# Scan and expert layer on one core: runs of eight in the corner products, split copies, six loads in flight, zero rows by GpSimd, and a new list

## The chip, the cores and the metric

One core of a Trainium2 chip runs the whole program. The metric is device microseconds of one execution. Three executions of the kernel before took 586.05, 586.7 and 592.21 us; the median is 586.7 us.

## The reference

The reference is a recurrent attention over 768 time steps for 4 batches and 8 heads of 40 channels, followed by a mixture of experts. Per step and head it keeps a 40 x 40 state:

```python
y[t] = r[t] @ state
Sa = state @ a[t]
state = state * w[t] - outer(Sa, b[t]) + outer(v[t], k[t])
```

The outputs of all heads form 3072 rows of 320 columns. Each row goes to the expert with the largest logit (8 experts with 320 x 1024 and 1024 x 320 weights, ReLU between, a capacity of 768 rows each), and its result is weighted by the softmax probability of that expert.

## The kernel before

The scan is done in 6 blocks of 128 steps (index `i`), each for two halves of the batches (`pr` = 0, 1) and in two chunks of 64 steps (`c` = 0, 1). Within a chunk the recurrence is a triangular system. A block has these steps, named as in the list:

- `load_w`, `load_a`, `load_kb`, `load_rv`, `load_v` (L457 to L495 and `unit`) bring the block's inputs into the buffers `px`, `a`, `kb`, `rv` and `vu`. Each such step is two DMAs, issued by SyncE (SP) through `Schedule.dma` (L156). The first load into a buffer has 128 rows, whose last rows are zeros in memory; a later load into the same buffer has 112 rows (the set `whole` remembers the buffers that have had a full load). Loads are spaced: each DMA waits until the third DMA before it has landed.
- `decay` scans `px` twice on VectorE (L503, L512) and multiplies `a` (L517); `decay_k` multiplies the two halves of `kb` (L522). The second half reads the last column of `gx`, which GpSimd sets to one (L427).
- `nn` and `kk` are products of `kb` and `a` on TensorE; their results are copied to `ns` and, masked, to `tk`.
- `inverse` (L587 to L830) inverts the triangular matrices: a transposition of `ns` (L791), a chain of small eliminations on VectorE (L638, L643), two corner products that are each two multiplications (L661) and a sum (L668, L670), and two transpositions (L680, L685). `unit` sets the buffer `nu` to the identity on ScalarE and reads a column of ones from `few`, which GpSimd sets (L434).
- `join`, `lower`, `lower_w` and `comb` join the inverted parts with products on TensorE. `take_n` makes four masked copies from `n1` to `yb` and `take_n1` two; both are one step in the list, on one engine.
- `chain`, `uT`, `turn`, `out`, `zz`, `iden` carry the state from chunk to chunk; `gate`, `logi`, `rout` prepare the routing.

The experts follow (`x`, `w`, `p`, `h`, `o` in the list), with weights loaded and split while the last blocks run, and take the last 200 us.

All steps are emitted in the order that `ORDER` gives, one text list for all engines, and each engine runs its own instructions in that order. In the list `name*2` is two steps of a name, `name/1` the second choice of engine for it (VectorE instead of ScalarE for copies, GpSimd instead of VectorE for multiplications), and `name~9` puts nine warm-up matmuls (L196, on TensorE, 128 x 512, whose results nobody uses) ahead of it. Instructions outside the list, as the memsets at the start (L425 to L445), are ordered by a planner, in the text's order unless one isn't ready. Before the first step the text clears buffers: PSUM on ScalarE, then on GpSimd the columns of the four `vu` buffers that `load_v` writes later, then `D`, `E`, `yq`, `yb`, `zs`, then the column of `gx`, then `mask` and `few`:

```python
    clear(*[flat(x) for x in free_["pp"] + free_["p1"]])
    for x in [x[:, :, :, C:3 * C] for x in free_["vu"]] + free_["D"] + free_["E"] + free_["yq"] + free_["yb"] + free_["zs"]:
        G.memset(x, 0.0)
    for x in free_["gx"]:
        G.memset(x[:, H * (P + 1):], 1.0)
...
            dma(U["vu"][half(x ^ pr), x, :, C:3 * C], vt[pr, q, x].rearrange("p (k y) -> p k y", k=4))
```

## Time and profile before

| what | value |
|---|---|
| median of three executions | 586.7 us (586.05 to 592.21) |
| the profiled execution | 590.8 us, span 589.1 us |
| TensorE busy | 521.2 us, 88% |
| VectorE busy | 413.9 us, 70% |
| ScalarE busy | 293.5 us, 50% |
| GpSimd busy | 160.8 us, 27% |
| mean granted TensorE clock | 0.992 |

The span is the time from the first to the last instruction of the profiled execution; some 1.7 us lie around it. A busy share is a mean over stages: the start (to about 57 us), the scan (to about 380 us) and the experts. In a timeline each row is a group of like instructions of one engine with its start and the time it covers; what stands in brackets is how long the engine stood idle before and what released it. PE is TensorE, PEld its weight loads, DVE VectorE, ACT ScalarE, POOL GpSimd, SP SyncE; SPq is the queue on which SP issues DMAs.

### The profile page before, as it was taken

The page shows a single profiled execution, that of the slowest core. Times are in us where ns is not written, and L with a number is a line of the kernel's source. Part 1 is how long each engine was busy: PE and PEld are TensorE (multiplying, and loading weights), DVE is VectorE, ACT ScalarE, POOL GpSimd, SP SyncE. Part 2 cuts the span into 40 slices and gives each one's busy share as a digit, 9 for nine tenths or more (in the row PEclk, how much of TensorE's full clock was granted, in tenths as well). Part 3 has the DMA queues.
Part 4 walks back from the last instruction along what each step waited for, and adds up shares of the span by engine and source line. Part 5 has one row for each costly group of instructions (what it writes and reads, how often), then busy time and mean ns, then how long its engine had stood idle before and what let it go on. Part 6 is the DMA issues. An engine that isn't in the chain of part 4 may idle for free.

```text
span 589.1 us, 24793 instructions
## 1 busy us (share of the span) xinstructions
PE 521.2 (88%) x11162; PEld 383.8 (65%) x11162; DVE 413.9 (70%) x665; ACT 293.5 (50%) x550; POOL 160.8 (27%) x181
## 2 busy tenths in 40 slices
PE   0587898999989899999798999799899999999994
PEld 0354477877877887878687788566665465555653
DVE  5886889779896988798899879657247256363340
ACT  3333656572786577357634453445345445273231
POOL 9014102340240223233202000412444441423203
PEclk9998999999999999999899999999999999999999
DMA  7754005332661534254221313675998877693301
GB/s 230 216 177 151 3 5 164 116 120 72 195 196 41 172 119 143 68 168 141 89 78 46 119 48 125 165 216 170 210 225 183 271 175 172 150 267 117 83 22 59
DMA packets 74760, 80.81 MB, mean 137 GB/s; under 512 B 31550, under 2 KB 55232, under 8 KB 74644
## 3 DMA queue, kind: packets, MB, share of 16 engines
q1 hardware_dynamic: 71316, 69.69, 41.4%
q0 software_dynamic: 3328, 9.44, 5.5%
q8 instruction: 89, 1.46, 1.0%
q14 instruction: 27, 0.22, 0.1%
HBM read 64.16 MB, written 10.09 MB: 126 GB/s over the span
## 4 chain that ended last, share of the span: by engine, by line
issue 20%; PE 15%; DVE 7%; POOL 6%; DMA 4%; ACT 2%; SPq 1%; POOLq 1%; DVEq 0%; ACTq 0%
PE pp L403 5%; PE pp L1624 3%; POOL out_dram L1499 3%; PE p L1493 3%; POOL a L1470 2%; DMA xT<-a 1%; DMA a<-xd,ri 1%; PE pp L885 1%; DMA out_dram<-tk,ri 1%; DVE vu L455 1%; DMA nt<-in_moe_w_dram 1%; DVE yq L661 1%; PE p L1126 1%; PE pp L570 1%; SPq L1609 1%
## 5 line engine op out<-in xcount | busy, mean ns | idle before, releaser
L522 POOL TENSOR_TENSOR kb<-kb,gx 104x1024 f32<-104x1024 f32 x13 | 33.4, 2576 | 80.7 <-DMA kb<-in_kb_dram 47.3
L196 PE MATMUL pp<-ident 128*128 128x512 f16 x148 | 41.8, 397 | 12.2 <-ACT pp L421 3.2
L403 PE MATMUL pp<-a,kb 64*64 64x64 f32 x1536 | 31.3, 229 | 20.9 <-DVE a L517 18.5
L403 PEld LDWEIGHTS pp<-a,kb 64*64 64x64 f32 x1536 | 26.8, 140 | 30.6 <-DVE a L517 21.0
L1470 POOL DMA_INDIRECT a<-xd,ri x26 | 30.3, 1166 | 58.3 <-DVE gs L1385 31.3
L1499 POOL DMA_INDIRECT out_dram<-tk,ri x23 | 25.9, 1126 | 61.3 <-ACT tk L1659 49.4
L403 PE MATMUL pp<-vu,bk 128*40 128x104 f32 (+1 forms) x768 | 38.2, 252 | 3.3 <-DVE vu L455 3.2
L143 ACT COPY vT<-pp 128x1024 f32<-128x1024 f32 x21 | 21.3, 1014 | 31.4 <-PE pp L885 28.7
L403 PEld LDWEIGHTS pp<-vu,bk 128*40 128x40 f32 x768 | 32.8, 117 | 6.1 <-DVE vu L455 4.3
L503 DVE TENSOR_TENSOR_SCAN gx<-px,z 104x1032 f32<-104x1032 f32 x12 | 29.2, 2430 | 8.5 <-DMA px<-in_w_dram 6.9
L517 POOL TENSOR_TENSOR a<-a,px 104x1024 f32<-104x1024 f32 x8 | 17.5, 2182 | 55.6 <-DVE px L512 30.1
L1624 PE MATMUL pp<-xT,z 128*128 128x448 f16 (+2 forms) x128 | 27.7, 306 | 5.4 <-DMA xT<-a 4.3
L1624 PE MATMUL pp<-xT,ns 128*128 128x448 f16 (+2 forms) x192 | 32.1, 306 | 0.0
L455 DVE TENSOR_TENSOR vu<-pp,mask 128x1024 f32<-128x1024 f32 x22 | 26.7, 1213 | 7.0 <-PE pp L403 4.9
L147 ACT ACTIVATE ns<-pp 32x256 f32<-32x256 f32 (+1 forms) x45 | 20.2, 449 | 22.3 <-PE pp L403 21.2
L143 ACT COPY zs<-pp 64x320 f32<-64x320 f32 x46 | 19.3, 419 | 23.9 <-PE pp L403 23.4
L196 PEld LDWEIGHTS <-ident 128*128 128x128 f16 x169 | 15.0, 100 | 24.1 <-issue 12.0
L403 PE MATMUL pp<-rv,vT 64*64 64x64 f32 x1536 | 28.4, 221 | 2.5 <-issue 1.3
L451 POOL TENSOR_SCALAR_AFFINE_SELECT tk<-tk 64x512 f32<-64x512 f32 x20 | 14.5, 726 | 57.5 <-ACT tk L448 46.6
L578 ACT ACTIVATE bk<-pp,few 128x320 f32<-128x320 f32 x48 | 22.5, 528 | 14.8 <-PE pp L570 14.5
L403 PE MATMUL pp<-yb,ns 128*64 128x64 f32 (+1 forms) x768 | 25.8, 229 | 3.7 <-ACT yb L147 3.6
L403 PEld LDWEIGHTS pp<-rv,vT 64*64 64x64 f32 x1536 | 24.9, 134 | 5.9 <-issue 2.2
(267 smaller groups left out, 1426.4 us busy)
## 6 DMA issues: line engine op xcount, KB each, us to landing
vu<-in_moe_w_dram SPq DMA_DIRECT2D x32, 320.0 KB
kb<-in_kb_dram SPq DMA_DIRECT2D x40, 224.0 KB
rv<-in_rv_dram SPq DMA_DIRECT2D x24, 256.0 KB
vu<-in_vt_dram SPq DMA_DIRECT2D x48, 128.0 KB
px<-in_moe_w_dram SPq DMA_DIRECT2D x12, 512.0 KB
xd<-x SPq DMA_DIRECT2D x24, 192.0 KB
px<-in_moe_w_dram SPq DMA_DIRECT2D x16, 256.0 KB
a<-in_a_dram SPq DMA_DIRECT2D x16, 224.0 KB
```

What stands on the lines that cost most here:

```text
L143: (e.copy if e is self.nc.scalar else e.tensor_copy)(out, in_)
L147: (e.mul if e is self.nc.scalar else e.tensor_scalar_mul)(out, in_, x)
L196: self.nc.tensor.matmul(x, self.spare[:, 0:P], self.spare[:, None, :].to_broadcast([P, 2, 2 * P]), start=True, stop=True, skip_group_check ...
L403: TT.matmul(out, l, r, start=start, stop=True, skip_group_check=True)
L455: V.tensor_mul(out, in_, m.to_broadcast(sh))
L503: V.tensor_tensor_scan(T["gx"][0:R, 0:H * (P + 1)][:, ::-1], T["px"][0:R].rearrange("p h t -> p (h t)")[:, ::-1], z2[0:R].rearrange("p h t ...
L522: engine().tensor_mul(x, x, g[:, :, None, half(c)].to_broadcast([R, H, 2, C]))
L578: A.activation(U["bk"][:, x].rearrange("p (a b) d -> p a b d", a=2), U["pi"][:, :, 0:4 * R].rearrange("p a (b y) -> p a b y", y=R)[:, :, : ...
L1470: nc.gpsimd.indirect_dma_start(out=xt(j)[:c].rearrange("p a c -> p (a c)"), out_offset=None, in_=src[:, :], in_offset=bass.IndirectOffsetO ...
L1493: nc.tensor.matmul(po[z], h(l, f + z), rr(f + z, 1)[:, 0], start=(f == 0 and m == 0), stop=(f == NF - n and m == 2), skip_group_check=True)
L1499: nc.gpsimd.indirect_dma_start(out=out_v[used[0] % (8 * E)][:, :], out_offset=bass.IndirectOffsetOnAxis(ap=ri.bitcast(U32)[:c, j, 1:2], ax ...
L1624: nc.tensor.matmul(s_["h", f + z][:, :n], l, rr, start=m % 7 == 0 and m < 14, stop=m >= 14)
```

## The change

- The first corner product is laid out anew and a step `corner_turn` is added to `inverse`: VectorE copies the 128 elements that the product reads in strides of 32 into `tmp`, in rows of eight. Both corner products then read all operands in runs of eight neighbouring elements; the second one is reordered in the same way.
- `take_n` and `take_n1` are two steps each, of half the copies, which the list can put on different engines.
- The first 24 load DMAs wait for the sixth before them instead of the third.
- Eight buffers (the four of `a`, one of the two of `kb`, three of the six of `px`) count as filled from the start, so that their first loads have 112 rows too; GpSimd sets rows 96 to 127 of each to zero, in the text just ahead of the memsets of `vu`.
- The list is a new one for the whole program: 1812 steps for 1794 (18 more, from the split and the added steps), and 146 warm-up matmuls for 169.

```diff
--- before.py
+++ after.py
 ORDER = """
-load_kb load_w decay0 load_kb load_a decay0 load_rv load_kb load_w decay_k0 load_a load_kb inverse_0 load_w decay_k0
-decay1 decay0 nn0~1 nn0 nn0~9 decay1 decay_k1 load_v decay1 kk decay_k1 decay0 unit nn0 nn1*2 kk/1 nn1 load_a
...
+load_w load_v unit load_kb decay0 decay_k0 load_w load_kb*2 decay0 decay_k0 load_rv load_w load_a decay1 load_a
+decay0 nn0 decay1 inverse_0 load_kb nn0 nn0~12 decay_k1 decay1 kk nn0 decay_k1 nn1*2 kk/1 decay0 nn1*2 inverse*2
+kk~3 iden1~4 inverse load_v iden0~3 iden0 inverse load_a iden1 inverse load_v kk/1 inverse*3 iden1~5 load_a inverse
+load_w inverse*3 load_rv inverse iden1 inverse*2 iden0 inverse*2 zz0~5 inverse*2 zz1~10 inverse*2 chain1 join_sw
+join/1 join decay0 load_kb decay_k0/1 join~9 load_kb decay0 iden0 decay_k0 join join~7 join*2 lower comb load_kb*2
+lower comb/1 comb~12 nn0~4 load_w decay1 comb/1 lower_w comb~5 tk_ decay1 decay_k1 inverse_0 nn0 decay1 comb nn0~6
+comb nn0 nn1~2 decay_k1 decay0 nn1 load_g nn1~3 nn1 unit chain1 chain0/1 chain0~2 kk inverse chain0 inverse*2 uT0~1
+inverse*2 load_w chain1 inverse uT0 inverse*4 kk/1 inverse*2 uT1 out0 uT1 zz0~1 out0/1 inverse out1~1 inverse out0
+inverse out1/1 out1 inverse out0 chain0 out0 out1 load_v turn0 out1 load_v chain0 inverse load_a iden0 chain0 zz1
...
@@ -156,8 +157,9 @@
     def dma(self, out, in_):
         x = (self.nc.scalar if self.queue.pop(0) == "A" else self.nc.sync).dma_start(out, in_)
         if self.spaced:
-            if len(self.loads) > 2:
-                self.tc.add_manual_dep(x.ins, self.loads[-3].name, LANDED, reason="loads are spaced")
+            n = 6 if len(self.loads) < 24 else 3
+            if len(self.loads) >= n:
+                self.tc.add_manual_dep(x.ins, self.loads[-n].name, LANDED, reason="loads are spaced")
             self.loads.append(x.ins)
 
     def load(self, fn):
@@ -421,6 +423,8 @@
                 A.copy(y, tmp[:, None, 0:256].to_broadcast(list(y.shape)))
 
     clear(*[flat(x) for x in free_["pp"] + free_["p1"]])
+    for x in free_["a"][:1] + free_["kb"][1:] + free_["px"][1:2] + free_["a"][1:2] + free_["px"][2:4] + free_["a"][2:]:
+        G.memset(flat(x)[96:], 0.0)
     for x in [x[:, :, :, C:3 * C] for x in free_["vu"]] + free_["D"] + free_["E"] + free_["yq"] + free_["yb"] + free_["zs"]:
         G.memset(x, 0.0)
     for x in free_["gx"]:
@@ -455,6 +459,8 @@
             V.tensor_mul(out, in_, m.to_broadcast(sh))
 
     whole = set()
+    for x in free_["a"][:1] + free_["kb"][1:] + free_["px"][1:2] + free_["a"][1:2] + free_["px"][2:4] + free_["a"][2:]:
+        whole.add(id(x))
 
     def prep(pr, i):
         T = {"pr": pr, "i": i}
@@ -647,18 +653,24 @@
         def eight(x, b, t, s, *dims):
             return skew(x, b * 528 + t * 32 + s, *dims)
 
+        def corner_turn():
+            V.tensor_copy(tmp[:, 0:P].rearrange("p (b j s) -> p b j s", b=2, j=8),
+                          skew(s_["nu"], 0, (528, 2), (1, 8), (32, 8)))
+
         def corner_mul(x):
             def go():
                 if x == 0:
                     s_["y"] = get("yq")
                 for b in range(2):
+                    y = flat(s_["y"])[:, 512 * b:512 * b + 512]
                     if x == 0:
-                        l = eight(s_["xu"], b, 8, 0, (32, 8), (0, 8), (1, 8))
-                        r = eight(s_["nu"], b, 0, 0, (0, 8), (1, 8), (32, 8))
+                        V.tensor_mul(y.rearrange("p (j t s) -> p j t s", j=8, t=8),
+                                     eight(s_["xu"], b, 8, 0, (0, 8), (32, 8), (1, 8)),
+                                     skew(tmp, 64 * b, (8, 8), (0, 8), (1, 8)))
                     else:
-                        l = eight(s_["nu"], b, 8, 8, (32, 8), (0, 8), (1, 8))
-                        r = skew(tmp, P + 64 * b, (0, 8), (1, 8), (8, 8))
-                    V.tensor_mul(flat(s_["y"])[:, 512 * b:512 * b + 512].rearrange("p (t j s) -> p t j s", t=8, j=8), l, r)
+                        V.tensor_mul(y.rearrange("p (t j s) -> p t j s", t=8, j=8),
+                                     eight(s_["nu"], b, 8, 8, (32, 8), (0, 8), (1, 8)),
+                                     skew(tmp, P + 64 * b, (0, 8), (8, 8), (1, 8)))
             return go
 
         def corner_sum(x):
@@ -691,12 +703,13 @@
             for z in range(2):
                 scale(two(y, z), x(z).rearrange("p (u x) t -> p u x t", x=2), mlo[:, z:z + 1])
 
-        def take_n():
-            y = s_["yb"] = get("yb")
-            for x in range(2):
-                for z in range(2):
-                    o = C // 2 * x + 16 * z
-                    scale(y[half(x), :, o:o + 16], s_["n1"][half(x), :, 0:16], mlo[half(x), z:z + 1])
+        def take_n(x):
+            if x == 0:
+                s_["yb"] = get("yb")
+            y = s_["yb"]
+            for z in range(2):
+                o = C // 2 * x + 16 * z
+                scale(y[half(x), :, o:o + 16], s_["n1"][half(x), :, 0:16], mlo[half(x), z:z + 1])
 
         def turned():
             return [(z, pr, pr * 16 + u, u) for u in range(16) for pr in range(2) for z in range(2)]
@@ -746,11 +759,12 @@
             for pr in range(2):
                 scale(x[half(pr)], s_["ntd"][half(1 - pr), pr * 16:pr * 16 + 16, :], mlo[half(1 - pr), 1:2])
 
-        def take_n1():
-            y = s_["yb"] = get("yb")
-            for x in range(2):
-                scale(y[half(x), :, 32 * x:32 * x + 32], s_["n1"][half(x)], mlo[half(x), 0:1])
-            put("nu", s_["nu"])
+        def take_n1(x):
+            if x == 0:
+                s_["yb"] = get("yb")
+            scale(s_["yb"][half(x), :, 32 * x:32 * x + 32], s_["n1"][half(x)], mlo[half(x), 0:1])
+            if x:
+                put("nu", s_["nu"])
 
         def comb_a():
             p = s_["p"] = get("pp")
@@ -797,6 +811,7 @@
         for s in range(1, ne - 1):
             for x in elim(s):
                 add(x, "V.2")
+        add(corner_turn, "V.4")
         for x in range(2):
             add(corner_mul(x), "V1.2", take=["yq"] * (1 - x))
             add(corner_sum(x), "V1.2", free=["yq"] * x)
@@ -805,7 +820,8 @@
         add = steps("join_sw")
         add(take_sw, "A.33 A.33|V.34 V.34", needs=[("ntd0", i)], take=["sw"], gives=("sw", i))
         add = steps("join")
-        add(take_n, "A.62 A.62 A.62 A.62|V.69 V.69 V.69 V.69", needs=[("n0", i)], take=["yb"])
+        for x in range(2):
+            add(lambda x=x: take_n(x), "A.62 A.62|V.69 V.69", needs=[("n0", i)], take=["yb"] * (1 - x))
         add(join_a, "P1.1", take=["pp"], free=["yb"])
         add(take_ja, "A.62 A.62|V.69 V.69", take=["yq"], free=["pp"])
         add(join_b, "P1.0", needs=[("sw", i)], take=["pp"], free=["yq", "sw"])
@@ -815,7 +831,8 @@
             steps("lower")(lambda pr=pr: lower(pr), "A.62 A.62|V.69 V.69", needs=[("ntd", i)], take=["nt"], gives=("lower", pr, i))
         steps("lower_w")(lower_w, "A.62 A.62|V.69 V.69", needs=[("ntd", i)], take=["sw"], gives=("lower", 2, i))
         add = steps("comb")
-        add(take_n1, "A1.04 A1.04|V1.2 V1.2", needs=[("n1", i)], take=["yb"], free=["nu"])
+        for x in range(2):
+            add(lambda x=x: take_n1(x), "A1.04|V1.2", needs=[("n1", i)], take=["yb"] * (1 - x), free=["nu"] * x)
         add(comb_a, "P1.3", take=["pp"], free=["yb"])
         add(take_a, "A1.04|V1.2", take=["yq"], free=["pp", "ns"])
         add(comb_b, "P1.4", needs=[("lower", x, i) for x in range(3)], take=["pp"], free=["yq", "sw"])
```

## Rows read from the trace of the kernel before

**Rows 1.** The page: busy time, share of the span and instructions by engine.
```profile
PE 521.2 (88%) x11162; PEld 383.8 (65%) x11162; DVE 413.9 (70%) x665; ACT 293.5 (50%) x550; POOL 160.8 (27%) x181
```

**Rows 2.** Table by stages: stage, length, busy of PE, PEld, DVE, ACT, POOL, PEclk, DMA, GB/s.
```profile
0.00:21.00 21.00, 0.88 (x13) 0.40 (x16) 12.48 (x16) 5.22 (x6) 14.44 (x58) 1.00 0.73 234
...
57.00:100.00 43.00, 36.44 (x1139) 28.30 (x1133) 37.28 (x52) 24.79 (x45) 2.18 (x1) 1.00 0.15 42
...
sum 323.00, PE 295.51 PEld 246.93 DVE 277.15 ACT 184.79 POOL 69.17; mean PE 49.25 PEld 41.15 DVE 46.19 ACT 30.80 POOL 11.53
```

**Rows 3.** Timeline of POOL at the start: start, length, engine, line, operation, tiles.
```profile
4.14 0.94 POOL L425 MEMSET vu<- 128x1024 f32 x1
...
5.07 2.72 POOL L425 MEMSET vu<- 128x1024 f32 x3
...
10.47 1.80 POOL L425 MEMSET yb<- 128x2048 f32 x1
...
12.79 0.09 POOL L427 MEMSET gx<- 128x1 f32 x1
```

**Rows 4.** Timeline of DVE, 0 to 32 us.
```profile
6.28 2.31 DVE L503 TENSOR_TENSOR_SCAN gx<-px,z 104x1032 f32<-104x1032 f32 x1 [3.85 <-DMA px<-in_w_dram]
...
12.91 1.23 DVE L522 TENSOR_TENSOR kb<-kb,gx 104x1024 f32<-104x1024 f32 x1 [0.33 <-POOL gx L427]
...
17.23 2.31 DVE L503 TENSOR_TENSOR_SCAN gx<-px,z 104x1032 f32<-104x1032 f32 x1 [3.07 <-DMA px<-in_w_dram]
19.45 1.20 DVE L517 TENSOR_TENSOR a<-a,px 104x1024 f32<-104x1024 f32 x1
...
31.06 1.98 DVE L791 STREAM_TRANSPOSE xu<-ns 128x1024 f32<-128x1024 f32 x1 [1.08 <-ACT ns L147]
```

**Rows 5.** Timeline of SP's DMA queue: the first load and the first of vu.
```profile
0.82 0.88 SPq L157 DMA_DIRECT2D kb<-in_kb_dram  x2
...
21.50 1.32 SPq L157 DMA_DIRECT2D vu<-in_vt_dram  x2
```

**Rows 6.** Timeline of PE: warm-up matmuls of the start.
```profile
21.77 4.02 PE L196 MATMUL pp<-ident 128*128 128x512 f16 x9
...
32.43 2.33 PE L196 MATMUL pp<-ident 128*128 128x512 f16 x10
```

**Rows 7.** Timeline of ACT: the masked copies of block 0.
```profile
47.31 2.68 ACT L147 ACTIVATE yb<-nu,few 64x512 f32<-64x512 f32 x4 [0.47 <-DVE nu L685]
...
60.53 2.32 ACT L147 ACTIVATE yb<-nu,few 64x1024 f32<-64x1024 f32 x2
```

**Rows 8.** DMA view, 0 to 80 us: GB/s in 40 slices of 2 us.
```profile
GB/s 6 316 245 255 244 257 279 225 272 181 251 189 215 212 159 230 175 108 118 229 170 217 235 276 192 277 158 0 0 0 8 0 0 8 0 8 0 4 8 0
```

**Rows 9.** Waits of SP's queue, 0 to 60 us: total, times, longest.
```profile
SPq L157 <- DMA kb<-in_kb_dram: 12.7, 16, 1.5
```

**Rows 10.** The corner multiplications' line: duration in ns, least, median, most.
```profile
L661 DVE TENSOR_TENSOR yq<-xu,nu x12: 1025/1056/1071, 37.3 to 310.1; 128x512 f32<-128x512 f32 x12
L661 DVE TENSOR_TENSOR yq<-nu,tmp x12: 1085/1104/1115, 40.6 to 313.7; 128x512 f32<-128x512 f32 x12
```

**Rows 11.** DVE groups by shape: count, busy us, mean ns, idle before.
```profile
L147 DVE TENSOR_SCALAR ns<-pp 32x256 f32<-32x256 f32 x18 | 7.6, 424 | 0.4
...
L147 DVE TENSOR_SCALAR ns<-pp 128x512 f32<-128x512 f32 x9 | 6.2, 687 | 4.0 <-PE pp L403 2.8 <-ACT vu L448 1.1
...
L1362 DVE TENSOR_TENSOR tm<-lane,sp 128x512 f32<-128x512 f16 x5 | 3.4, 687 | 0.0
...
L147 DVE TENSOR_SCALAR yb<-nu,few 64x1024 f32<-64x1024 f32 x4 | 3.0, 747 | 0.1
...
L631 DVE COPY nu<-xu 128x28 f32<-128x28 f32 x6 | 1.1, 191 | 0.3
```

**Rows 12.** The chain that ended last, 262 to 330 us: start, length, what.
```profile
309.13 2.04 DVE yq L661 x2
```

**Rows 13.** Table by stages of line L196 alone, the whole span: its last line.
```profile
sum 589.00, PE 48.01 PEld 15.01; mean PE 3.43 PEld 1.07
```

More of the change, by code (lines that the diff above doesn't have):

```diff
@@ new lines @@
+inverse_0 iden0 unit gate1 comb decay_k1/1 zz1~2 comb turn0 gate1/1 gate1 zz1 chain0~2 decay1 comb chain0 chain1*2
+nn0 nn0/1 uT0 decay1/1 uT0 turn0/1 chain1 nn0*2 out0~2 chain1/1 nn1 tk_ load_kb decay_k1/1 out0 load_v nn1/1 nn1*2
+uT1 inverse*2 turn1 kk inverse uT1 out0 kk/1 inverse iden0 out0 inverse out0 load_rv zz0 iden0 inverse logie0
+inverse chain0 out1 turn1/1 inverse*3 chain0 load_v logie0 chain0~2 turn0 inverse*2 chain0 inverse out1/1 inverse
+out1 inverse load_w zz1*2 inverse turn0 uT0 out1*2 iden1 chain1 inverse uT0 inverse out0 logie1 tk_ inverse load_a
@@ new lines @@
+load_v inverse*2 chain1 out0 chain1 decay0 iden1 gate1 kk~3 out0 chain1 out0 kk zz0 out0 join*2 iden0 logie1 iden0
+chain0 logie0/1 chain0/1 join_sw join~1 gate1 uT1 join load_v decay0*2 turn1 load_kb uT1 join*2 decay_k0/1 turn1
+logie1 join load_kb gate0~1 logie1/1 gate0 out1 gate0 comb/1 iden1~3 load_a logie0 out1/1 comb lower load_w lower
+unit decay_k0/1 comb decay1 comb gate0 out1 turn0~2 lower_w load_kb nn0 load_kb load_v decay1 inverse_0 out1 iden1
+nn0 turn0 comb*2 fill zz1 decay1 out1 zz1 turn1~2 decay_k1 comb decay_k1 chain0 nn1 chain0 chain1 load_rv uT0 nn1
@@ new lines @@
+decay0 kk/1 join_sw join*2 out0 gate1 out0 turn1 iden0~1 join iden0 uT1 gate0*2 load_v decay0 join zz0 load_kb
+logie0 turn1/1 uT1/1 out1 chain0 gate0 join load_kb comb out1/1 out1 gate0 load_rv iden1 comb/1 chain0 lower out1
+logie0/1 gate0 unit decay0/1 zz1 decay_k0/1 out1 zz1 logie0 decay_k0/1 comb turn1~3 decay1 iden1 load_kb gate1
+lower_w lower/1 decay1 comb comb~2 turn1 chain1 inverse_0 tk_ decay_k1/1 gate1/1 comb load_kb logie1 gate1 logie0/1
+chain0 comb turn0 logie1/1 chain0 load_v nn0 chain1 nn0/1 logie1 decay1/1 nn0 chain1 load_rv nn0 uT0 decay_k1/1
@@ new lines @@
+gate0 turn0 out1/1 logie0 join load_kb gate0*2 out1 join load_rv join gate0 comb/1 out1 gate0 load_v out1 logie0*2
+lower iden1 comb decay_k0 decay0/1 lower_w decay1 comb load_kb lower decay1 comb inverse_0 nn0*2 logie1 logie0/1
+comb gate1~3 turn1 load_kb logie1 comb decay1 iden1 zz1 comb hand_px decay_k1 logie1 chain0~1 zz1 gate1*2 chain1 tk_
+nn1 chain0 chain1/1 logie1 nn0 nn1/1 nn0 decay_k1/1 uT0 nn1 kk uT0/1 nn1 turn1 kk/1 hand_px hand_z chain1 out0
+chain1 unit uT1 out0/1 out0 inverse*2 uT1 inverse iden1 out0 load_rv out0 inverse iden1 out1 inverse zz0 iden0
@@ new lines @@
+inverse out1/1 inverse*2 chain0*2 out1 iden0 turn0 route inverse hand_a inverse zz1 inverse zz1 inverse chain0 out1
+inverse*2 tk_ load_v out1 inverse*2 chain1 inverse chain0 turn1 chain1 uT0 kk inverse hand_gx uT0 chain1 out0
+inverse kk turn0 out0/1 out0 zz0 inverse turn1 gate1 chain1 out0*2 uT1 chain0 uT1 chain0 inverse iden1 gate1 out1
+iden1 gatf0 out1 join/1*2 gatf0*2 join_sw join*2 route*2 out1*2 join out1 iden0 route turn0 logif1 load_v join*2
+turn0 logif0 gatf0/1 comb/1 comb gatf1 iden0 hand_kb lower/1 logif1 lower/1 logif0 comb~1 gatf0 route comb/1 logif1
@@ L114 @@
+o7_0 o4_2 p7*5 o7_3 p7 o7_1*2 o7_2*2
 """
```

130 lines of the change are left out of this document (49 added, 81 removed).

## The prediction, made before the change was run

> **What bounds the kernel now.** I read the page's shares first: TensorE (PE) is busy for 88% of the span [rows 1]. That is an average over three stages, so the second view is the table by stages [rows 2]. In the first 21 us PE works 0.88 us and VectorE (DVE) 12.48 us; that stage waits for loads and for DVE. From 57 to 380 us, five and a half blocks of the scan, PE is busy 295.5 us and DVE 277.2 us of 323, so both are near full and neither alone is the bound. After 380 us the experts follow; the change touches them only through the list, and I leave them at nothing, since their dense PE work stays as it is.
>
> The third view is the timeline of the start, engine by engine [rows 3 to 7]. What ends it is one chain: first scan of `px` at 6.28 us when its load lands, multiplications of `kb`, second scan at 17.23 us (3.07 us of waiting for its load), multiplication of `a` ending at 20.65 us, PE, ScalarE (ACT), and the inverse's first transposition at 31.06 us [rows 4, 6, 7]. The inverse and what follows it up to the first chain step have no other block to hide behind.
>
> **The start: zero rows and loads.** Eight memsets over 32 partitions (four `a`, one `kb`, three `px`) stand in the text ahead of the memsets of `vu`, and GpSimd (POOL) ran its memsets in the order of the text [rows 3]. A memset of 1024 columns over 128 partitions takes 0.91 us from start to start (2.72 us for three), one of 2048 columns 1.80 us [rows 3]. Over 32 partitions no row exists. By columns the eight cost 7 x 0.91 + 1.80 = 8.2 us; by partitions a quarter, 2.0 us. I take 8.2: the rows that exist go by columns, and none shows a gain by partitions.
>
> The Trainium skill ("GPSIMD Engine Reference", section 2 Architecture) says that each of eight cores owns 16 partitions and that an instruction completes when all are done. By it a memset over 32 partitions would take as long as one over 128, and the sum would be the 8.2 us.
>
> So the memset of the first `vu` would end at 4.14 + 0.94 + 8.2 = 13.3 us and that of `gx`'s last column, 12.79 us now, would come at 21.0 us. Two things wait for them. First, the new list puts `load_v` second. It writes the columns that the memset clears, so its two DMAs must wait, and SyncE (SP) issues in order: all the loads behind it (kb, px, kb, kb, rv, px, a, a, kb) stand until 13.3 us, where now the first `load_v` goes at 21.50 us, behind ten other loads and long after its memset [rows 3, 5]. Second, the multiplication of `kb`'s second half waits for `gx`'s last column, as it already did for 0.33 us [rows 4].
>
> The loads then: from `vu` to the first `a` 3592 KB lie on the queue (256 + 512 + 452 + 512 + 448 + 512 + 452 + 448; 512 is 128 rows of 1024 words, and 112 rows are an eighth less). With three in flight the start ran at 234 GB/s [rows 2]; the best slice of it reached 316 [rows 8]. Six in flight should come between; at 290 that is 12.4 us, with 1.5 us of latency `a` lands at 27.2 us (26.2 at 316, 30.2 at 234). DVE has by then done its `kb` products (the second from 21.0 us) and the second scan, both of which precede `a` in the list, and ends `a` at 28.4 us instead of 20.65.
>
> From there to the inverse took 10.4 us. Now 12 warm-up matmuls instead of 9 stand between the first two products of PE; the nine took 4.02 us, 0.45 each, where ten of them took 2.33 us eleven microseconds later [rows 6]; the engine had stood still before the first. Three more cost 0.7 us at the later pitch (1.3 at the first). The inverse begins at 28.4 + 10.4 + 0.7 = 39.5 us, 8.4 us late (7 to 12).
>
> The copy of `ident` into `nu`, now third in the list, ends with a read of a column that POOL writes behind all this, at about 22.5 us. ACT stands until then, and behind it only the first `ns` copies, wanted at 29 us: nothing.
>
> **The inverse.** The four corner multiplications take 1.056 and 1.104 us by their medians [rows 10]; each has one operand read in strides of 32 or 8 elements. A product of the same 512 columns with unit strides took 0.687 us [rows 11]. With runs of eight I take that: 2 x 0.37 + 2 x 0.42 = 1.58 us saved per inverse, at least zero. The added copy reads 128 elements in strides of 32: over 0.19 us, which 28 such elements took [rows 11], and under 0.19 + 128 x 1.056/512 = 0.45; I take 0.36. With a gap of 0.03 that leaves 1.2 us per inverse, and in block 0 all of it is on the path.
>
> The row shows strided reads at half again the price. The Trainium skill ("SBUF — State Buffer", section Door 1: The DMA port swizzle) has lines of 16 bytes of which two accesses must hit the same one; a run of eight floats meets that and the added copy does not, so by it the sum is the same 1.58 and the copy stays at the strided price.
>
> **The copies in two steps.** `take_n` is four ACT copies of 2.68 us, `take_n1` two of 2.32 [rows 7]. In block 0 the new list gives one half of each to DVE, which copies a half of `take_n1` in 0.75 us [rows 11]. If both run side by side the path loses 1.34 + 1.16 = 2.5 us; at worst nothing, if DVE is held by its scan. Start in all: 8.4 - 1.2 - 2.5 = **+4.7 us**.
>
> **Blocks 1 to 5.** Corner: 5 x 1.2 = 6 us less on DVE, and it can lie on the path there: the chain of waits runs through the corner multiplications of the last block [rows 12]. The new list gives DVE 4 `nn` copies where the old gives 9: 5 x (0.69 + 2 x 0.42) = 7.7 us less [rows 11]; it takes four multiplications back from POOL, +4.8 at 1.20 each [rows 4]. I leave the other exchanges at nothing; they go both ways. DVE: -8.9 us. Warm-up matmuls fall from 169 to 146, by 21 of them past the start; 48.0 us for all 169 [rows 13] is 0.28 each, 5.9 us of PE. What of these 14.8 us is on the path? The engines are 91% and 86% busy, in order, each waiting for the other [rows 2]; I take a third, **-4.9 us**; the ends are nothing and all, and a new order can also lose some 5.
>
> **Sum.** +4.7 - 4.9 = -0.2 us. The profiled execution took 590.8 us (span 589.1), 0.7% over the median of 586.7; the difference is put on the median, 586.5; I write 586.
>
> **Rivals.** (1) The start is in time, because the zero rows cost a quarter or the memsets of `vu` and `gx` run ahead of them. Then `a` lands when its 4108 KB have come, 0.8 + 14.2 + 1.3 = 16.3 us, ends at 17.5, and the inverse begins at 17.5 + 11.1 = 28.6, 2.5 us earlier: -2.5 - 3.7 - 4.9 = -11.1, **576 us**. For it: the order of a few POOL rows is not that of the text, so a planner stands behind it. Against it: all memsets of this function are in order [rows 3].
> (2) Slower: the late loads stay late. With the queue closed for 12 us, all of block 1's loads move too; if six in flight move no more than three (234 GB/s), `a` lands at 30.2 and the start is +11, -3.7 with the gains in block 0; and no third comes back, as PE is the bound behind it at 91%. +7.3, with the three warm-ups at their first pitch +8: **595 us**. It decides from a landing of `a` past 29 us. For it: SP waits for landings now at 16 of its `kb` issues alone [rows 9], so landings set the pace there; against it: from 57 to 100 us the DMA engines are busy 15% of the time [rows 2], so lost loads can be made good.
> (3) Corner multiplications as slow as before, the change not doing what it says: 1.58 us back on the path in block 0 and a third of 7.9 in the others, 4.2 us: **590 us**.
>
> **How the numbers follow.** The forecast, a late start won back, 580 to 592 by its bounds: 0.45. Rival 1: 0.27. Rival 2: 0.21. Rival 3: 0.07. About 1%, 5.9 us, is what a measurement of this kernel can tell from no change. Faster: 0.24 of rival 1 and 0.12 of the forecast's lower end, 0.36. Slower: 0.19 of rival 2 and 0.05 of the other two, 0.24. Within: 0.40. The range leaves out a tenth at each end: 574 to 597.
>
> **What would show it.** POOL: the eight memsets, 8 us between 4 and 13 us, and `gx`'s memset at 21. SP: a gap in the issues from about 2 to 13.3 us, released by POOL. DVE: `a` ending at 28 us, transposition at 39. Corner rows of 0.69 us and a copy of 0.36. In block 0 `yb` copies on both engines at once. From the inverse's start to the end of the scan some 9 us less than now. It is wrong if the first `vu` load goes before 8 us, if the inverse begins before 34 us, or if the time from the first inverse to the end moves by more than 15 us.

## The result, and the profile after

The changed kernel took 594.9 us (median of 4, 592.39 to 597.9), the kernel before 586.7 us beside it. The ratio is 1.0126, interval 1.008 to 1.0172: slower by 1.3%. The profiled execution took 596.1 us, span 594.4, for 590.8 and 589.1 before; the mean granted clock of TensorE was 0.975 for 0.992.

The page: busy times by engine, and the granted clock in 40 slices. They answer to [rows 1].

```profile
PE 520.2 (88%) x11139; PEld 387.1 (65%) x11139; DVE 400.4 (67%) x659; ACT 300.1 (50%) x570; POOL 166.4 (28%) x189
...
PEclk9999799999989999799999999899999999999998
```

VectorE lost 13.5 us of work, TensorE one, and the span grew by 5.3 us: the change did take work away, and the time went into waiting. So the next views are of the start, engine by engine, as before. GpSimd (answers to [rows 3]):

```profile
4.25 0.95 POOL L427 MEMSET a<- 32x1024 f32 x1
...
5.44 1.80 POOL L427 MEMSET kb<- 32x2048 f32 x1
...
12.68 3.62 POOL L429 MEMSET vu<- 128x1024 f32 x4
...
21.33 0.09 POOL L431 MEMSET gx<- 128x1 f32 x1
```

SyncE's queue (answers to [rows 5]), and what it waited for in the first 40 us:

```profile
0.82 0.88 SPq L158 DMA_DIRECT2D px<-in_w_dram  x2
13.66 1.31 SPq L158 DMA_DIRECT2D vu<-in_vt_dram  x2
...
25.30 3.44 SPq L158 DMA_DIRECT2D a<-in_a_dram  x4
```

```profile
SPq L158 <- POOL vu L429: 11.9, 1, 11.9
```

VectorE's timeline (answers to [rows 4]):

```profile
19.82 1.23 DVE L528 TENSOR_TENSOR kb<-kb,gx 104x1024 f32<-104x1024 f32 x1 [12.86 <-DMA kb<-in_kb_dram]
...
25.76 2.31 DVE L509 TENSOR_TENSOR_SCAN gx<-px,z 104x1032 f32<-104x1032 f32 x1
31.57 1.23 DVE L523 TENSOR_TENSOR a<-a,px 104x1024 f32<-104x1024 f32 x1 [3.51 <-DMA a<-in_a_dram]
...
42.89 1.93 DVE L805 STREAM_TRANSPOSE xu<-ns 128x1024 f32<-128x1024 f32 x1
```

One chain is to be seen. The zero rows take GpSimd from 4.25 to 12.6 us, the memset of the first `vu` ends behind them, the queue stands for 11.9 us for it, `a` lands at 31.5 us, and the inverse begins at 42.89 us instead of 31.06.

The corner's two lines and the added copy (duration in ns: least, median, most; answers to [rows 10]) show that the work itself became as cheap as hoped:

```profile
L667 DVE TENSOR_TENSOR yq<-xu,tmp x12: 682/686/2680, 49.4 to 315.5; 128x512 f32<-128x512 f32 x12
...
L671 DVE TENSOR_TENSOR yq<-nu,tmp x12: 683/688/693, 53.9 to 318.1; 128x512 f32<-128x512 f32 x12
...
L657 DVE COPY tmp<-nu x6: 259/272/275, 49.1 to 314.6; 128x128 f32<-128x128 f32 x6
```

The last view is a table of four stretches of the scan; the column behind the busy times is the granted clock.

```profile
59.90:66.70 6.80, 5.56 (x69) 4.23 (x70) 5.67 (x7) 3.39 (x6) 0.00 (x0) 0.51 0.34 114
169.10:172.50 3.40, 3.40 (x73) 2.90 (x72) 2.60 (x6) 1.72 (x2) 1.67 (x1) 0.51 0.58 175
240.80:247.60 6.80, 6.80 (x102) 5.77 (x106) 3.01 (x6) 2.98 (x8) 1.83 (x1) 0.51 0.22 68
295.40:298.80 3.40, 3.40 (x101) 3.27 (x100) 2.67 (x7) 1.40 (x4) 0.90 (x1) 0.51 0.02 5
```

In 20.4 us of the scan TensorE ran at the lower of its two levels (1.2 for 2.4 GHz); in the kernel before it was 6.8 us, 3.4 of them at the first joining of block 0. Ahead of each of these stretches it had stood still: 3.59, 1.28, 2.17 and 0.91 us. The first is in block 0, ahead of the first product of joining:

```profile
55.44 2.10 PE L198 MATMUL pp<-ident 128*128 128x512 f16 x9 [0.97 <-ACT zs L144]
61.14 3.68 PE L405 MATMUL pp<-yb,ns 128*64 128x64 f32 x64 [3.59 <-ACT yb L148]
```

### The profile page after: what moved, and what is told of

Read it like the earlier page. It is cut to its first block, busy times and chain, and to the rows that moved or that the text cites. A ratio compares the mean times of both kernels' runs of the same rounds, so it can differ in the third digit from the quotient of the medians.

```text
span 594.4 us, 24764 instructions
## 1 busy us (share of the span) xinstructions
PE 520.2 (88%) x11139; PEld 387.1 (65%) x11139; DVE 400.4 (67%) x659; ACT 300.1 (50%) x570; POOL 166.4 (28%) x189
## 4 chain that ended last, share of the span: by engine, by line
PE 28%; issue 23%; POOL 7%; DVE 7%; ACT 3%; another core or an unknown queue 1%; DMA 1%; POOLq 1%; DVEq 0%; ACTq 0%
PE pp L405 16%; POOL out_dram L1516 4%; PE pp L1641 3%; PE pp L902 2%; POOL a L1487 2%; PE pp L576 1%; PE p L405 1%; PE p L1510 1%; PE pp L1034 1%; DVE vu L459 1%; PE p L940 1%; PE p L1143 1%; DMA px<-in_moe_w_dram 1%; POOL vT L1487 1%
## 5 line engine op out<-in xcount | busy, mean ns | idle before, releaser
L1641 PE MATMUL pp<-xT,vu 128*128 128x448 f16 (+2 forms) x192 | 44.1, 323 | 0.0
L528 POOL TENSOR_TENSOR kb<-kb,gx 104x1024 f32<-104x1024 f32 x12 | 26.5, 2211 | 57.2 <-PE pp L576 24.6
L198 PE MATMUL pp<-ident 128*128 128x512 f16 x129 | 36.2, 397 | 4.3 <-ACT ns L148 1.7
L148 ACT ACTIVATE ns<-pp 32x256 f32<-32x256 f32 (+1 forms) x60 | 27.0, 449 | 22.6 <-PE pp L405 21.4
L405 PE MATMUL pp<-rv,vT 64*64 64x64 f32 x1536 | 30.4, 225 | 4.1 <-issue 3.4
L1510 PEld LDWEIGHTS <-nt 128*128 128x128 f16 (+1 forms) x288 | 23.8, 101 | 14.5 <-issue 3.8
L144 ACT COPY vT<-pp 128x1024 f32<-128x1024 f32 x21 | 21.3, 1012 | 20.4 <-PE pp L902 16.5
L459 DVE TENSOR_TENSOR vu<-pp,mask 128x1024 f32<-128x1024 f32 x20 | 24.3, 1215 | 9.9 <-PE pp L405 9.9
L518 DVE TENSOR_TENSOR_SCAN px<-px,z 104x1032 f32<-104x1032 f32 x12 | 29.5, 2461 | 0.4
L1646 ACT ACTIVATE nt<-pp 128x448 f16<-128x448 f32 (+1 forms) x28 | 13.1, 497 | 33.1 <-PE pp L1641 28.4
L1641 PE MATMUL pp<-xT,xu 128*128 128x448 f16 (+2 forms) x128 | 27.5, 307 | 2.0 <-DVE px L1649 2.0
```

Source lines behind the costliest of these rows:

```text
L148: (e.mul if e is self.nc.scalar else e.tensor_scalar_mul)(out, in_, x)
L198: self.nc.tensor.matmul(x, self.spare[:, 0:P], self.spare[:, None, :].to_broadcast([P, 2, 2 * P]), start=True, stop=True, skip_group_check ...
L405: TT.matmul(out, l, r, start=start, stop=True, skip_group_check=True)
L459: V.tensor_mul(out, in_, m.to_broadcast(sh))
L518: V.tensor_tensor_scan(T["px"][0:R].rearrange("p h t -> p (h t)"), T["px"][0:R].rearrange("p h t -> p (h t)"), z2[0:R].rearrange("p h t -> ...
L528: engine().tensor_mul(x, x, g[:, :, None, half(c)].to_broadcast([R, H, 2, C]))
```

## The experiments

Theory 1: the late start is the loss. Theory 2: the start is made good, and the stretches at the lower clock eat the gain. Theory 3: the new list is itself worse by the block. All kernels below ran beside the kernel before, whose median was 588.0 to 589.8 us there; the ratio is to it. The table gives where each kernel stands in its profiled execution, in us: the first transposition of the inverse, and the add that ends joining in block 0 and in block 5 (the last line of `take_jb`). "Vu first" is the kernel of experiment 1. The places come from one execution of each kernel, and executions of one kernel lie 4 to 11 us apart, so a few us late in the scan can be the execution's and not the edit's; the ratios rest on four to nineteen executions of each.

| kernel | inverse begins | joining ends, block 0 | block 5 | median us | ratio, interval |
|---|---|---|---|---|---|
| before | 31.06 | 58.41 | 331.04 | | 1 |
| changed | 42.89 | 69.09 | 334.98 | 594.9 | 1.0126 (1.008 to 1.0172) |
| 1 vu first | 34.97 | 57.32 | 315.11 | 579.9 | 0.9875 (0.9803 to 0.9946) |
| 2 no zero rows | 33.80 | 58.85 | 320.16 | 582.7 | 0.9882 (0.9823 to 0.9941) |
| 3 three in flight | 45.00 | 70.19 | 332.09 | 592.5 | 1.006 (1.0023 to 1.0097) |
| 4 before, new corner | 29.53 | 54.18 | 326.32 | 583.5 | 0.9891 (0.982 to 0.9962) |
| 5 more warm-ups | 44.49 | 68.75 | 336.79 | 603.5 | 1.0271 (1.0216 to 1.0327) |
| 6 load_v later | 36.80 | 63.26 | 321.40 | 587.7 | 0.9972 (0.993 to 1.0013) |
| 7 vu first, old corner | 36.74 | 64.31 | 333.81 | 591.3 | 1.0047 (1.0009 to 1.0086) |
| 8 load_v later, zero rows by need | 29.70 | 52.86 | 315.66 | 580.0 | 0.9889 (0.9816 to 0.9961) |
| 9 before, six in flight | 28.04 | 55.88 | 331.02 | 591.4 | 1.0067 (1.003 to 1.0103) |
| 10 vu first, copies on ScalarE | 33.93 | 60.16 | 323.34 | 589.8 | 1.0021 (0.9978 to 1.0065) |
| 11 before, zero rows | 36.14 | 63.45 | 339.22 | 600.0 | 1.0216 (1.0139 to 1.0293) |
| 12 load_v later, no zero rows | 28.13 | 52.88 | 313.02 | 576.4 | 0.9809 (0.974 to 0.9877) |
| 13 changed, 128 rows | 40.29 | 64.41 | 326.00 | 591.7 | 1.0036 (0.999 to 1.0083) |
| 14 vu first, warm-ups gone | 35.34 | 60.56 | 324.60 | 588.1 | 0.9994 (0.9958 to 1.003) |

**1. The vu memset first.**

```diff
+    G.memset(cleared[0], 0.0)
+    for x in free_["px"][1:2] + free_["kb"][1:]:
         G.memset(flat(x)[96:], 0.0)
     for x in free_["gx"]:
         G.memset(x[:, H * (P + 1):], 1.0)
...
```

> The changed kernel with GpSimd's zeroing alone put in another order: the memset of the first vu tile first, then the zero rows of px and kb (two memsets), then the ones of gx, then the other zero rows, then the rest. Nothing else differs. Theory 1 (the late start is the loss: zero rows ahead of the vu memset and of the ones of gx, and load_v second in the list, hold the queue of SP until 13.7 us): the first vu load is issued near 5.5 us, the load of a lands by 22 to 25 us, the first transposition of the inverse comes at 31 to 35 us instead of 42.9, and the time falls by 6 to 10 us from 594.9, to 585 to 589. Theory 2 (the granted clock, which falls to 0.50 in 24 us of the changed kernel and in 7 of the one before, is the loss): the start comes earlier just the same but the later stretches at 0.50 stay, and the time stays at 591 to 596. Theory 3 (the new list is itself worse by the block): as theory 2 but with the granted clock back at 0.99.

The order of GpSimd's memsets alone turned a loss of 1.3% into a gain of 1.25%. VectorE and, for joining, TensorE:

```profile
23.18 1.22 DVE L527 TENSOR_TENSOR a<-a,px 104x1024 f32<-104x1024 f32 x1 [3.75 <-DMA a<-in_a_dram]
...
34.97 1.94 DVE L809 STREAM_TRANSPOSE xu<-ns 128x1024 f32<-128x1024 f32 x1
```

```profile
51.86 2.08 PE L405 MATMUL pp<-yb,ns 128*64 128x64 f32 x64 [1.70 <-ACT yb L148]
```

The start came 7.9 us earlier, the time fell by 2.5%, 14.7 us, where 6 to 10 were expected: TensorE stood still for 1.70 instead of 3.59 us ahead of joining, kept the full clock and did it in 2.08 us for 3.68, and up to the end of block 5 only 3.4 us are at the lower level. The kernel before had this joining at the lower level too:

```profile
50.14 3.54 PE L403 MATMUL pp<-yb,ns 128*64 128x64 f32 x64 [2.21 <-ACT yb L147]
```

Theory 1 stands, and theory 2 as it was put falls, since the stretches did not stay. Theory 3 falls: the same list is 1.25% faster than the old one once the start is in time. How much of the gain is the start and how much the clock that came back with it, this experiment does not part.

**2. No zero rows** (the loop of memsets and the buffers put in `whole` ahead removed, so first loads bring 128 rows).

> The changed kernel without the zero rows: GpSimd clears none, and the first loads bring all 128 rows again; six in flight and the new list stay. Theory 1 (late start): the vu memset is done near 5.1 us, the ones of gx near 13, the load of a lands by 24 us, the inverse begins at 31 to 35 us, the time is 585 to 589; it differs from the kernel in which the vu memset only comes first by what 112 rows for 128 are worth, at most 2 us. Theory 2 (clock): 591 to 596 with stretches at 0.50 of 20 us or more. Theory 3 (list): 591 to 596 at a clock of 0.99.

The start came as theory 1 had it, and the time fell below its range. The inverse begins 1.2 us before that of experiment 1 although more bytes are moved; the intervals of the two ratios overlap.

**3. Three in flight.**

```diff
-            n = 6 if len(self.loads) < 24 else 3
+            n = 3
```

> The changed kernel with three loads in flight throughout, where the first 24 had six; zero rows, 112 rows and the list stay. If six in flight are worth nothing (the loads are bound by the bytes at 219 to 234 GB/s): the load of a lands within 1 us of where it did, and the time stays within 2 us of 594.9. If six in flight hide the latency of single loads: a lands 3 us or more later, and the time rises by 2 to 5 us.

The product with `a` began at 32.46 us for 31.57. So six in flight with 112 rows are worth 0.9 us at `a`, as the first expectation had it. The intervals of the two ratios overlap, so no difference in the time is shown.

**4. The kernel before with the new corner** (`corner_turn` and the two multiplications; one more `inverse` per block in the list).

> The kernel before with the new corner alone: the copy of the corner's turn and the two multiplications that read runs of eight; start, masked copies and order stay, with one more step of the inverse in the list of each block. The corner saves 0.37 to 0.42 us a multiplication and spends 0.27 on the copy, about 1.3 us an inverse with four multiplications. Theory 1 (the corner is a gain and the start alone the loss): 580 to 586, with the first inverse 1.3 us shorter. Theory 2 (gains on DVE turn into idle time of PE and stretches at 0.50): 586 to 590. If the corner is on no path: 586 to 588.

583.5 us is 1.1% faster, 6.4 us, but by another way than the sum: in the profiled execution block 0 ends 4.2 us earlier and blocks 1 to 5 take 272.1 us for 272.6. So in the old order the trace shows nothing of the corner by the block. The two traces account for half of the gain alone: their executions are 3.1 us apart, and both lie some 4 us over their medians.

**5. More warm-ups in the changed kernel.**

```diff
-join/1 join decay0 load_kb decay_k0/1 join~9
+join/1 join decay0 load_kb decay_k0/1 join~25
```

In the same way one `chain0` of block 3 became `chain0~9` and one `zz0` of block 4 `zz0~4`.

> The changed kernel with more warm-up multiplications where TensorE's idle time stood ahead of a fall of the granted clock: 25 for 9 ahead of the first step of joining in block 0 (3.6 us idle ahead of 59.9 to 66.7 us at 0.50), 9 for none ahead of the chain's multiplication of block 3 (2.2 us idle ahead of 240.8 to 247.6), 4 for none ahead of a multiplication with tk in block 4 (0.9 us idle ahead of 295.4). Start, loads and order stay as changed. The start as the whole loss: still 592 to 596, the first transposition of the inverse still near 42.9 us. The clock as a second part of it: the stretches at 0.50 in the scan fall from 20.5 to about 7 us, half of the 13.5 us comes back where TensorE is the bound, 3 to 6 us, and the time is 588 to 592.

```profile
57.81 5.56 PE L196 MATMUL pp<-ident 128*128 128x512 f16 x25 [0.97 <-ACT zs L142]
63.29 2.08 PE L403 MATMUL pp<-yb,ns 128*64 128x64 f32 x64
```

No stretch of the scan is at the lower level any more, joining runs in 2.08 us, and yet block 5 ends 1.8 us later and the time is 8.5 us longer (by the ratios). In block 3 the nine came behind the wait instead of into it (idle 2.42 us, then 2.10 us of warm-ups), so they cost what they take. Behind block 5, where nothing was edited, the profiled execution lost a further 3.6 us; why is not shown. As a cure the theory of the clock falls; as a cause of its own it isn't settled by this, since the added work costs too.

**6. load_v later** (moved in the list from second place to behind the second `load_a`; GpSimd as in the changed kernel).

> The changed kernel with the first load_v moved in the list from second place to behind the second load_a; the zero rows stay ahead of the vu memset and of the ones of gx. It parts the two ways in which the zero rows can delay the start. If SP's queue, closed behind load_v until 13.7 us, is what counts: the loads go out from 1 us, the load of a lands near 20 us, and the product with a waits for nothing but the multiplication with gx at 21.3, so it begins at 23 to 25 instead of 31.6; the first transposition at 34 to 36, the time 582 to 587. If VectorE's wait for the ones of gx (21.3 us) counts as much: the product begins at 29 or later and the time is 589 to 593.

```profile
21.45 1.23 DVE L526 TENSOR_TENSOR kb<-kb,gx 104x1024 f32<-104x1024 f32 x1 [10.59 <-POOL gx L429]
...
24.96 1.20 DVE L521 TENSOR_TENSOR a<-a,px 104x1024 f32<-104x1024 f32 x1
```

The two walls come apart. The ones of `gx` hold the product with `a` to 24.96 us, 5.5 us after that of before; the closed queue held it for another 6.6 us, to 31.57. The time, 587.7 us, lies just above the first range.

**7. Vu first with the old corner.**

> The kernel with the vu memset first (579.9 us) with the old corner put back: its two multiplications of 1.06 and 1.10 us a half for 0.69, no copy of 0.27, one step of the inverse fewer in each block's list; nothing else differs. If the corner counts in full in block 0 and in part later, as the sum had it (1.3 us in block 0 and a third of it in each of five): 582 to 585. If VectorE is on the path in every block: 586 to 588. If the corner is on no path of the new order and the order alone makes it faster by the block: 579 to 581.

All three expectations were too small: 1.7%, 10 us. VectorE's groups, the multiplications (count, busy us, mean ns, idle before):

```profile
L669 DVE TENSOR_TENSOR yq<-nu,tmp 128x512 f32<-128x512 f32 x12 | 13.2, 1140 | 0.2
L669 DVE TENSOR_TENSOR yq<-xu,nu 128x512 f32<-128x512 f32 x12 | 12.2, 1059 | 0.1
```

That is 9.2 us more on VectorE than in experiment 1 (8.4 and 7.8), less 1.6 for the copies. Block 0 ends 7.0 us later, 1.8 of it from the start, and again 20.5 us of the scan are at the lower level. Each of blocks 1 to 5 takes longer than in experiment 1, by 1.1 to 5.6 us; but the two traces are of the longest execution of the one kernel (597.2 us) and the shortest of the other (578.0), 19 us apart where the ratios put 10 us between them. So in the new order the time answers to the corner in full, 10 us for 7.6 us of work; that it does so in every block is what one execution of each shows.

**8. load_v later, zeroing in the order of need.**

> The kernel with the vu memset first, one step further: the first load_v behind the second load_a, and GpSimd's zeroing in the order in which the loads need it, with the ones of gx third (near 7 us) and the first vu memset behind the rows of the first a. Theory of the start: the load of a lands 2 us sooner than with the vu memset first, the product with a begins near 20 to 21 us for 23.2, the first transposition near 32 for 35.0, and the time falls by a further 1 to 3 us to 576 to 579. If from 580 on other waits set the path: no change, 579 to 581.

The inverse began 5.3 us sooner than in experiment 1, block 5 ended level with it: the gain was lost between blocks 2 and 4. One place shows, in VectorE's timeline of this kernel and of experiment 1:

```profile
213.96 2.16 DVE L520 COPY g<-gx 104x8 f32<-104x8 f32 x1
```

```profile
217.59 0.16 DVE L520 COPY g<-gx 104x8 f32<-104x8 f32 x1
```

The same copy took 2.0 us longer, and from 220.6 us TensorE was at the lower level for 6.8 us, which in experiment 1 it was not. Beside the longer copy GpSimd did a multiplication of `kb`; beside that of experiment 1 it did none, between one that ended at 214.56 us and one that began at 219.83 (more in the last section):

```profile
213.56 2.52 POOL L532 TENSOR_TENSOR kb<-kb,gx 104x1024 f32<-104x1024 f32 x1 [5.26 <-DMA kb<-in_kb_dram]
```

**9. The kernel before with six in flight** (the changed line of `Schedule.dma` alone).

> The kernel before with six loads in flight for the first 24 in place of three; all of 128 rows, nothing else. In the kernels that ran, six in flight with 112 rows moved 246 to 284 GB/s between 16 and 32 us and six with 128 rows (the kernel without zero rows) 239 to 384 between 12 and 24. If it is the number in flight that counts, the load of px that the second scan waits for 3.07 us lands sooner, the product with a begins at 16 to 18 us for 19.45, the first transposition near 28 to 29.5 for 31.06, and the time is 583 to 586. If the loads go no faster, or the gain is lost later: 585 to 589.

The start answered (product with `a` at 16.55 us), the time did not: slower by 0.7%, outside both ranges. At the end of block 5 of the profiled execution nothing is left of the 3.0 us. The table of the stretch from 8 to 16 us, this kernel and the kernel before (the last two columns are the DMA engines' busy share and GB/s):

```profile
8.00:16.00 8.00, 0.00 (x0) 0.00 (x0) 7.89 (x9) 0.00 (x0) 7.21 (x23) 1.00 1.04 380
```

```profile
8.00:16.00 8.00, 0.00 (x0) 0.00 (x0) 5.76 (x8) 0.00 (x0) 7.09 (x23) 1.00 0.78 251
```

**10. Vu first with block 0's masked copies all on ScalarE** (`join/1` and `comb/1` of block 0 became `join` and `comb`).

> The kernel with the vu memset first (579.9 us) with the masked copies of block 0 all on ScalarE, where the list gives one half of each to VectorE; the other blocks stay. If both halves run side by side, as the sum had it (2.5 us): the end of the first block's joining comes about 1.3 us later, the combination 1.2 more, 581 to 584 in all. If block 0 has slack behind it: 579 to 581.

```profile
49.48 2.68 ACT L146 ACTIVATE yb<-nu,few 64x512 f32<-64x512 f32 x4 [0.46 <-DVE nu L699]
```

The four copies took 2.68 us, where experiment 1 had two of 1.32 us beside two on VectorE. The term was right; the time moved by 1.5%, 8.6 us, far more than expected. TensorE stood still for 3.72 us ahead of joining, where it had been 1.70, and from 50.7 us was at the lower level for 6.8 us: joining took 3.68 us for 2.08, the seven warm-ups behind it 2.48 for 1.69. Joining ended 2.8 us later although the inverse had begun 1.0 us sooner, block 5 8.2 us later.

**11. The kernel before with the zero rows alone.**

> The kernel before with the zero rows alone: GpSimd's eight memsets ahead of those of vu, and the first loads of these tiles with 112 rows; three in flight and the old list, in which load_v comes behind two loads of a. It shows what the zero rows cost where they do not close SP's queue: the multiplication of kb's second half waits for the last column of gx until 21.3 us for 12.91, the product with a begins at 24 to 25 for 19.45, the first transposition at 35 to 37 for 31.06. Theory of the start: the time rises by 3 to 6 us, to 590 to 594. If a late start is made good in the blocks: 586 to 589.

```profile
21.45 1.23 DVE L526 TENSOR_TENSOR kb<-kb,gx 104x1024 f32<-104x1024 f32 x1 [8.60 <-POOL gx L429]
...
24.96 1.20 DVE L521 TENSOR_TENSOR a<-a,px 104x1024 f32<-104x1024 f32 x1
...
36.14 1.98 DVE L795 STREAM_TRANSPOSE xu<-ns 128x1024 f32<-128x1024 f32 x1 [0.65 <-ACT ns L147]
```

The places came as expected; the time rose by 2.2%, more than twice the 5.1 us of the start. Nothing of a late start is made good in the old order either.

**12. load_v later, no zero rows** (on GpSimd the ones of `gx` first, the first `vu` memset second).

> The kernel with load_v behind the second load of a (580.0 us) without the zero rows: all loads of 128 rows, six in flight, the ones of gx first on GpSimd and the first vu memset second. If loads of 112 rows move fewer bytes a second (262 GB/s at 16 DMA engines all busy for 327 with 128 rows) by as much as they save: the product with a begins within 1 us of 18.4 and the time stays at 578 to 582. If the narrower loads are the slower ones: 16 to 17.5 us, and 576 to 579 where the start still counts.

The product with `a` began at 15.69 us, and the kernel is the fastest of all: 576.4 us, 1.9% under the kernel before.

**13. The changed kernel with loads of 128 rows** (memsets and queue as changed).

```diff
-            y = slice(0, 112 if kind != "rv" and id(T[kind]) in whole else P)
+            y = slice(0, P)
```

> The changed kernel with its first loads of 128 rows; the eight memsets of zero rows stay where they are on GpSimd (now without a use), so SP's queue stays closed to 13.7 us and the ones of gx stay at 21.3. It tells whether the landing of a, 4.3 us later than the sum had it, lies in the loads of 112 rows (262 GB/s with all 16 DMA engines busy, for 327 to 380 with 128). If it does: the product with a begins at 27 to 29 us for 31.6, the first transposition at 38.5 to 40.5 for 42.9, the time 590 to 593. If the rows are not it: 31 us and 593 to 597.

The stretch from 18 to 30 us, when all loads of the start are under way: three in flight with 112 rows (experiment 3), six with 112 (changed), six with 128 (this one).

```profile
18.00:30.00 12.00, 0.00 (x0) 0.00 (x0) 7.21 (x6) 0.25 (x1) 6.35 (x20) 1.00 0.71 222
```

```profile
18.00:30.00 12.00, 0.00 (x0) 0.00 (x0) 7.20 (x6) 0.25 (x1) 6.67 (x20) 1.00 1.04 260
```

```profile
18.00:30.00 12.00, 0.00 (x0) 0.00 (x0) 8.08 (x7) 0.25 (x1) 7.30 (x20) 1.00 0.99 348
```

With the DMA engines busy all the time 112 rows move 260 GB/s and 128 rows 348. An eighth less to move at three quarters of the rate is slower: the product with `a` began at 29.02 us for 31.57, and the time lies between the changed kernel and the kernel before. The edit gives 128 rows to the later loads of the scan too, so the start answers for the rows alone and the time does not quite.

**14. Vu first without the nine warm-ups ahead of joining in block 0** (`join~9` became `join`).

> The kernel with the vu memset first (579.9 us) without the nine warm-up multiplications ahead of the first step of joining in block 0: TensorE then stands still for some 3.8 us ahead of it, as in the changed kernel. If the granted clock falls to 0.50 there and the delay is carried through the blocks: the first joining takes 3.7 us for 2.1, its end comes 1.5 to 3.5 us later, and the time is 582 to 588. If the fall costs only what it shows in block 0 and later blocks make it good: 579 to 581.

```profile
53.53 3.65 PE L403 MATMUL pp<-yb,ns 128*64 128x64 f32 x64 [5.72 <-ACT yb L146]
```

After 5.72 us of standing still TensorE did joining in 3.65 us for 2.08. An operation of VectorE's inverse (the copy into `tmp`) also took 1.9 us longer here than its like, where in experiment 1 one took 0.6 longer, so not all of the 3.2 us by which block 0 ended late is the clock's: 0.4 lie ahead of the inverse, 1.3 in that operation, 1.6 in joining. They were 9.5 us by block 5, and 1.2%, 7 us, in the time.

## Why the prediction was wrong

The forecast was 586 us, no change; 594.9 lies in the range, in the case of the second rival, at its 595. By the steps:

- **Zero rows on GpSimd:** right. 8.2 us were forecast, 4.25 to 12.6 us is 8.35; `vu` was to be done at 13.3 and its load went at 13.66; `gx` was put at 21.0 and came at 21.33. They go by columns, as [rows 3] had it.
- **The landing of `a`, "at 290 that is 12.4 us, with 1.5 us of latency `a` lands at 27.2 us (26.2 at 316, 30.2 at 234)": the step that failed.** It landed at 31.5, past the outer bound. The rate between three in flight and the best slice was taken from loads of 128 rows [rows 2, 8]. Half of the eight loads up to `a` had 112, and with these six in flight move 260 GB/s; 3592 KB (3.68 million bytes; the sum took a KB for 1000 bytes, which is 0.3 us) at 260 are 14.1 us, 29.3 with the latency. The other 2.2 us are bytes that the sum left out. From the first issue of `vu` to the landing (the last two columns are the DMA engines' busy share and GB/s):

```profile
13.66:31.50 17.84, 0.00 (x0) 0.00 (x0) 7.20 (x6) 0.25 (x1) 11.01 (x26) 1.00 0.91 237
```

237 GB/s over 17.84 us are 4.2 million bytes, 0.5 million more than lay up to `a`: loads issued behind it were moved beside it. At 260 GB/s they are 2.1 us. By the same sum experiment 13 (3848 KB at 348) would land `a` at 26.5, and its product began at 29.0; there too some 0.5 million bytes more were moved (292 GB/s from 13.68 to 28.95 us), 1.5 of the 2.5 us.
- **From there to the inverse:** right. 10.1 us from the end of that product to the transposition, 11.1 forecast. With `a` 4.3 us later than forecast the inverse began 11.8 us late and not 8.4.
- **Corner:** right in size. 0.686 and 0.688 us for a forecast 0.687, the copy 0.27 for 0.36, 1.3 us an inverse for 1.2.
- **Copies in two steps:** right (1.32 us on ScalarE beside 0.88 on VectorE for 2.68), and experiment 10 shows that they are on the path.
- **"-1.2 - 2.5" won back in block 0:** up to the end of joining that is 2.5 us, since 1.16 lie in the copies of `take_n1` behind it. It came to 1.1 us in the changed kernel (26.2 us from the inverse's begin to the end of joining, 27.35 before), to 5.0 in experiment 1 (22.35). Between the two lie one corner multiplication that took 2.68 us for 0.69 (1.4 us more than the like delay in experiment 1), joining at half the clock, 1.6 us, and the seven warm-ups behind it, 0.9. The delay was not in the sum. Of the clock, the kernel before had joining at 3.54 us already; that experiment 1 did it in 2.08 is a gain that no term held. Start in all: 10.7 us late at the end of joining, 5.9 forecast at that place.
- **Blocks 1 to 5, a third on the path, -4.9 us:** with the 1.16 us of `take_n1` it is -6.1 for this stretch, and it came to -6.7 us (265.9 us for 272.6), in spite of 13.6 us at the lower clock. The nearness is in part luck: in the kernels of the new list with the new corner the stretch took from 257.8 us (experiment 1, -14.8) to 268.0 (experiment 5, -4.6). That the -14.8 equals the 14.8 us of work that the prediction counted is one execution's figure.
- **Experts at nothing:** +1.4 us.

The sum is 10.7 - 6.7 + 1.4 = 5.4 us, the spans differ by 5.3; the medians differ by 8.2, and how the profiled execution stands to its median accounts for the rest. Against the forecast the start missed by 4.8 us, 3.4 of them up to the inverse, the blocks by -0.6 and the experts by 1.4.

**The rivals.** The second decided as it said, by a landing past 29 us, and gave the time; of its reasons, that six move no more than three is true within 0.9 us for 112 rows only, and that nothing is won back behind it is not. That its 595 met 594.9 is luck: its start of 7.3 to 8 us was 10.7, and its blocks of 0 were -6.7. The first rival, a start in time at 576 us, is what experiment 12 built, without zero rows: 576.4 us (experiment 8, with them, 580.0). Its sum met this by luck too: the inverse began 2.9 us earlier for 2.5, but the stretch of blocks 1 to 5 was 12.5 us shorter, where 4.9 and a part of the 3.7 were counted.

What stays open is why a delay in block 0 grows. In the new order 14.8 us of start (from experiment 12 to the changed kernel) are 18.5 us of time, and 3 us of delay behind the start (experiments 10 and 14) became 7 to 9. Most of the longer runs hold more stretches at the lower clock, but experiment 13 (591.7 us) has 3.4 us of them up to block 5, no more than experiment 1, and taking them away (experiment 5) did not bring the time back. A delay also changes which operations of VectorE meet a multiplication of GpSimd's (last section); how much of the growth that makes is not shown.

## What to carry to other kernels

A setup instruction on an idle engine is on the path as soon as an in-order queue issues a transfer that waits for it: put such setup in the order in which the transfers need it, and look at what stands behind the first waiting issue. Moving fewer bytes is a gain only if the rate stays; read GB/s beside the DMA engines' busy share before and after. Price a part in the order in which it will run: the same corner was worth 6.4 us in one list and 10 us in the other. And where one operation takes longer than its like, look at what the other engines did in that time.
